# Banded attention and a Sinkhorn mixture of experts: keys loaded in an order in which each query tile's 256 keys are two stretches of 128 adjacent columns

## The chip, the cores and the metric

The kernel runs on one core of one Trainium2 chip. The time is the device time of one execution in microseconds. Runs of an unchanged kernel agree within about 0.1% here (three runs from 2232.98 to 2233.5 us).

## The reference, cut to what matters

```python
# q, k, v: [4, 8, 768, 64] float32; n_global = 8, n_local = 96
scores = (q @ k.T) / sqrt(64)
rel = pos[:, None] - pos[None, :]
is_global = pos[None, :] < n_global
is_local = (rel >= 0) & (rel < n_local)
dist = where(is_global & ~is_local, n_local, abs(rel))
scores = where(is_global | is_local, scores - slope[h] * dist, -1e9)
a = exp(scores - max(scores)); a = a / (sum(a) + 1e-9)
x = a @ v                       # -> [3072, 512]
P = exp(x @ w_gate - max); 8 times: rows to sum 1, columns to sum 1, times N / E
out = sum over e of P[:, e] * (relu(x @ w1[e]) @ w2[e])   # 8 experts, 512 -> 1024 -> 512
```

A query needs only the 96 keys up to itself and the first 8 keys of the sequence. For a tile of 128 queries these lie among the tile's own 128 keys, the last 96 keys of the tile before, and the first 32 keys (`MAX_GLOBAL`, `G` in the code): 256 keys.

## The kernel before, in words

The work of the attention is cut into 32 items. An item is one batch, one half of the sequence (three tiles of 128 queries; half 0 or half 1) and two heads side by side in the 128 columns. Items 0 to 3 are half 0, 4 to 7 half 1, and so on; four items make a unit, and there are eight units. Each item has three groups, one for each query tile, with both heads; the groups are counted through as `t`, 96 in all.

For an item, the queries (three blocks of 128 x 128), the keys and the values are loaded by DMA, all issued from the SP queue (`load_qk`, `load_v`). Even items use a region of the tile `scratch` that is there from the start (`early_raw`), odd items a tile of the pool `f_raw`; so each has one buffer, and the loads of item n+2 wait until item n has used them. `load_pair` lays keys and values out alike. In half 0 there are four blocks: block 0 is made of the first 32 keys and the last 96 of tile 1, blocks 1 to 3 are the three tiles. In half 1 there are six: for each query tile one block of the first 32 keys and the last 96 of the tile before, and one with its own tile. Tiles 0 to 5 of the sequence appear partly twice by that.

`prepare` turns queries and keys: PE transposes each block into a PSUM tile `tp` (line 89 by way of `InOrder`), ACT copies it out as the high part (`qh`, `kh`, L248), DVE subtracts to get the low part (`ql`, `kl`, L249). It runs in three parts: the queries, four key blocks, and in half 1 two more key blocks; after the last part the queries and keys of item n+2 are asked for. `scores` makes three products for each group and head (low and high parts), `softmax` adds the scaled bias table on DVE (L296) and takes the exponential on ACT (L300), `turn` transposes the weights (`t_ps`, copied out on ACT at L322), and `values` multiplies them with the value blocks into `o_ps`. After the third group the values of item n+2 are asked for (`flush`).

The bias tables come from `distances` (DVE, at the very start, before a branch on the values of `n_global` and `n_local`) and `scale_bias`: for each head a table of 128 columns (first tile) and one of 256. Heads 0 and 1 are scaled on DVE, the others on POOL (L159). They lie in the tile `acc`, which the expert part later uses as its accumulator.

PE's order is the program's order. The tile framework sets the order of the other engines and of the SP queue from dependencies and from its own estimate of times. From unit 1 on, `between` mixes work of expert 0 into PE's stream (`filler`: `h_ps`, `y_ps`, stored by way of `y_sb` to `ys`), and POOL prepares operands of the later experts (`oh`, `ol`), which the SP queue stores to `op_m` in DRAM. After about 345 us the attention is over; the rest of the time is expert products with nothing of the attention in them.

The order of the work around the change, in `unit`:

```python
for t in range(u * per, (u + 1) * per, CHUNK):      # CHUNK = 2
    self.ahead(range(t + AHEAD, t + AHEAD + CHUNK))  # scores and softmax of later groups
    self.flush()                                     # values products, load_v(n + 2)
    turned = [(t + c, self.turn(t + c)) for c in range(CHUNK)]
    between(CHUNK)                                   # expert 0, stores
    ...
    for c in range(CHUNK):
        between(1)
        self.prepare(t + AHEAD + NG + 1 + c)         # transposes, load_qk(n + 2)
```

Of the kernel before, what the change touches and what calls it, by code (L numbers as in the profile page):

```python
# [12 lines left out]
ALU = mybir.AluOpType  # L13
# [22 lines left out]
GROUPS = (((0, 0), (1, 0)), ((0, 1), (1, 1)), ((0, 2), (1, 2)))  # L36

# [54 lines left out]
class Banded:  # L92

    SLOTS = 8 * len(GROUPS)
    RAW = UT * P + 4 * UT * P

    SCRATCH = RAW + 2 * P

    def __init__(self, tc, q, k, v, early, scratch):

        self.tc, self.nc = tc, tc.nc
        self.q, self.k, self.v = q, k, v
        self.H, self.D = q.shape[1], q.shape[3]
        H, nb = self.H, 3 * self.H * P
        self.bias1 = early[:, 0:2 * H * P].rearrange("p (h c) -> p h c", h=H)
        self.bias0 = early[:, 2 * H * P:nb].rearrange("p (h c) -> p h c", h=H)
        self.early_raw = scratch[:, 0:self.RAW]
        self.d1 = early[:, nb:nb + 2 * P]  # L110
        self.d0 = early[:, nb + 2 * P:nb + 3 * P]
        self.work = [(b, half, g) for b in range(q.shape[0]) for half in range(2) for g in range(H // 2)]
        self.pending = []
        self.sums, self.inv, self.outs = {}, {}, {}
        self.pe = InOrder(tc)
        nb += 3 * P
        self.early_pT = early[:, nb:nb + 4 * P].rearrange("p (c k) -> p c k", c=4)
        assert nb + 4 * P <= early.shape[1]
        self.warm = scratch[:, self.RAW:].bitcast(mybir.dt.bfloat16)
        self.qk, self.vs, self.ready, self.scored = {}, {}, {}, {}  # L120

    def open(self, ctx, ident, idle):

        tc = self.tc
        self.ident, self.idle = ident, idle
        self.raw = ctx.enter_context(tc.tile_pool(name="f_raw", bufs=1, side="right"))
        self.opd = ctx.enter_context(tc.tile_pool(name="f_opd", bufs=2, side="right"))
        self.wrk = ctx.enter_context(tc.tile_pool(name="f_wrk", bufs=AHEAD + CHUNK, side="right"))
        self.ps = ctx.enter_context(tc.tile_pool(name="f_ps", bufs=2, space=PSUM))

    def distances(self, ng, nl):

        tc, nc, G = self.tc, self.nc, MAX_GLOBAL
        d1, d0 = self.d1, self.d0
        with tc.tile_pool(name="f_tmp", bufs=1) as tmp:
            rel, isl, isg = position_tiles(nc, tmp, P, 0, 2 * P, ng, nl, "d1")
            m = tmp.tile([P, 2 * P], F32, name="m1")
            nc.vector.tensor_scalar(out=m, in0=isl, scalar1=-BIG, scalar2=BIG, op0=ALU.mult, op1=ALU.add)
            nc.vector.tensor_scalar(out=m[:, 0:G], in0=isg[:, 0:G], scalar1=-BIG, scalar2=BIG, op0=ALU.mult, op1=ALU.add)
            nc.vector.tensor_tensor(out=d1, in0=isl, in1=rel, op=ALU.mult)  # L140
            nc.vector.tensor_scalar(out=d1[:, 0:G], in0=isg[:, 0:G], scalar1=nl, scalar2=None, op0=ALU.mult)
            nc.vector.tensor_tensor(out=d1, in0=d1, in1=m, op=ALU.add)
# [4 lines left out]
            nc.vector.tensor_tensor(out=d0, in0=isl, in1=rel, op=ALU.mult)  # L147
            nc.vector.tensor_scalar(out=isl, in0=isl, scalar1=-1.0, scalar2=1.0, op0=ALU.mult, op1=ALU.add)
            nc.vector.tensor_tensor(out=m0, in0=m0, in1=isl, op=ALU.mult)
            nc.vector.tensor_tensor(out=d0, in0=d0, in1=m0, op=ALU.add)  # L150

    def scale_bias(self, g):

        nc, H, D = self.nc, self.H, self.D
        engine = nc.vector if g == 0 else nc.gpsimd
        for h in (2 * g, 2 * g + 1):
            c = -(D ** 0.5) * 2.0 ** (-8.0 * (h + 1) / H)
            for bias, d in ((self.bias0, self.d0), (self.bias1, self.d1)):
                self.tc.keep_in_program_order(engine.tensor_scalar(out=bias[:, h], in0=d, scalar1=c, scalar2=None, op0=ALU.mult))  # L159
# [13 lines left out]
    def raw_tile(self, n, first, width):  # L173


        if n % 2 == 0:
            t = self.early_raw[:, first * UT * P:(first + width) * UT * P]
        else:
            t = self.raw.tile([P, width * UT * P], F32, name=f"raw{width}")
        return t.rearrange("p (t c) -> p t c", c=P)  # L180

    def load_keys(self, dst, src, half, cols):
        nc, D, G = self.nc, self.D, MAX_GLOBAL
        if half == 0:
            nc.sync.dma_start(out=dst[:, 1:1 + UT, cols], in_=src[:, 0:UT])
        else:
            nc.sync.dma_start(out=dst[:, 1::2, cols], in_=src[:, UT:2 * UT])
            nc.sync.dma_start(out=dst[G:, 0::2, cols], in_=src[G:, UT - 1:2 * UT - 1])
            nc.sync.dma_start(out=dst[0:G, 0::2, cols], in_=src[0:G, 0:1].broadcast_to([G, UT, D]))
# [7 lines left out]
    def load_pair(self, dst, src, n):  # L197

        nc, D, G = self.nc, self.D, MAX_GLOBAL
        b, half, g = self.work[n]  # L200
        for t, cols in self.heads(src, n):
            self.load_keys(dst, t, half, cols)
        if half == 0:
            both = src[b, 2 * g:2 * g + 2].rearrange("j s d -> s j d")
            block = dst[:, 0].rearrange("p (j d) -> p j d", j=2)
            nc.sync.dma_start(out=block[0:G], in_=both[0:G])
            nc.sync.dma_start(out=block[G:], in_=both[P + G:2 * P])

    def load_qk(self, n):
# [3 lines left out]
        t = self.raw_tile(n, 0, 3)  # L213
# [3 lines left out]
        self.load_pair(k_r, self.k, n)  # L217
        self.qk[n] = q_r, k_r

    def load_v(self, n):  # L220
        if n >= len(self.work):
            return
        self.vs[n] = self.raw_tile(n, 3, 2)
        self.load_pair(self.vs[n], self.v, n)
# [5 lines left out]
    def prepare(self, t):  # L230
# [3 lines left out]
        if n >= len(self.work):  # L234
            return
        nc = self.nc
        if part == 0:
            self.ready[n] = tuple(self.opd.tile([P, w * UT, P], F32R, name=name)
                                  for name, w in (("qh", 1), ("ql", 1), ("kh", 2), ("kl", 2)))
        q_r, k_r = self.qk[n]  # L240
        qh, ql, kh, kl = self.ready[n]
        nk = self.key_blocks(self.work[n][1])[0]
        src, hi, lo, n0, n1 = ((q_r, qh, ql, 0, UT), (k_r, kh, kl, 0, 4), (k_r, kh, kl, 4, nk))[part]
        if n1 > n0:
            tp = self.turned("tp")
            for t in range(n0, n1):
                self.pe.transpose(out=tp[:, t - n0], in_=src[:, t], identity=self.ident)
            nc.scalar.copy(out=hi[:, n0:n1], in_=tp[:, 0:n1 - n0])  # L248
            nc.vector.tensor_tensor(out=lo[:, n0:n1], in0=tp[:, 0:n1 - n0], in1=hi[:, n0:n1], op=ALU.subtract)  # L249
        if part == 2:  # L250
            self.load_qk(n + 2)

    def scores(self, ts):
# [3 lines left out]
        banks = [self.ps.tile([P, CHUNK, 2 * P], F32, name=f"s_ps{j}", tag=f"s{j}", bufs=1) for j in range(2)]  # L257
        s_lists, terms = [], []
        for c, t in enumerate(ts):
            n, group = divmod(t, len(GROUPS))  # L260
            blocks = self.key_blocks(self.work[n][1])[1]
# [15 lines left out]
    def softmax(self, t, s_list):  # L277
# [5 lines left out]
        blocks = self.key_blocks(half)[1]  # L283
# [6 lines left out]
        for u, (j, i) in enumerate(GROUPS[group]):  # L290
            h = 2 * g + j
            nb = len(blocks[i])
            bias = self.bias0[:, h] if nb == 1 else self.bias1[:, h]
            pv = p_sb[:, u, 0:nb].rearrange("p a c -> p (a c)")
            views.append(pv)
            nc.vector.tensor_tensor_reduce(out=pv, in0=s_list[u], in1=bias, scale=-(D ** -0.5), scalar=3.0e38,  # L296
# [13 lines left out]
    def blocks(self, n, group):  # L310
        slots = self.key_blocks(self.work[n][1])[1]
        return [(u, a, j, i, slots[i]) for u, (j, i) in enumerate(GROUPS[group]) for a in range(len(slots[i]))]

    def turn(self, t):
# [6 lines left out]
        pT = self.wrk.tile([P, 4, P], F32, name="pT", bufs=1) if t % 2 else self.early_pT  # L321
# [668 lines left out]
def kernel(  # L990
# [68 lines left out]
```

## Time and profile before

| | |
|---|---|
| median of three runs | 2233.35 us (2232.98 to 2233.5) |
| the profiled execution | 2235.71 us |
| its span, first to last instruction | 2233.9 us |
| mean granted TensorE clock | 0.990 |
| busy share PE / PEld / DVE / ACT / POOL | 98% / 81% / 61% / 34% / 50% |

PE is the matrix engine, PEld its weight loads, DVE the vector, ACT the scalar, POOL the general engine; SPq is the queue of the SyncE engine, which issues the DMAs. In a row of the timeline stand start and duration in us, engine, line, operation, what is written and read, how many; in brackets the idle time of the engine before it and what ended that. A row of waits reads: who waited, for whom, us in total, how often, the longest. Matmuls overlap, so the spacing of two starts tells more of the cost of one than its duration.

### The profile page before, as it was taken

The page shows a single profiled execution, that of the slowest core. Times are in us where ns is not written, and L with a number is a line of the kernel's source. Part 1 is how long each engine was busy: PE and PEld are TensorE (multiplying, and loading weights), DVE is VectorE, ACT ScalarE, POOL GpSimd, SP SyncE. Part 2 cuts the span into 40 slices and gives each one's busy share as a digit, 9 for nine tenths or more (in the row PEclk, how much of TensorE's full clock was granted, in tenths as well). Part 3 has the DMA queues.
Part 4 walks back from the last instruction along what each step waited for, and adds up shares of the span by engine and source line. Part 5 has one row for each costly group of instructions (what it writes and reads, how often), then busy time and mean ns, then how long its engine had stood idle before and what let it go on. Part 6 is the DMA issues. An engine that isn't in the chain of part 4 may idle for free.

```text
span 2233.9 us, 29587 instructions
## 1 busy us (share of the span) xinstructions
PE 2194.8 (98%) x10887; PEld 1817.9 (81%) x10887; DVE 1358.9 (61%) x2382; ACT 769.0 (34%) x1562; POOL 1126.3 (50%) x1050
## 2 busy tenths in 40 slices
PE   8999998999999999999999999999999999999999
PEld 5888886778888888888888888888888888888887
DVE  5555556866566656655666666566556665666665
ACT  6676763223222322223222222222232232222221
POOL 5575575545454545445544545454555455544540
PEclk8999999999999999999999999999999999999999
DMA  6566554111111111162111111111521111111111
GB/s 157 160 168 180 150 161 162 39 48 48 57 48 57 48 57 48 57 221 89 49 49 55 51 54 48 57 48 57 167 88 47 57 48 57 48 51 54 50 46 49
DMA packets 224842, 177.68 MB, mean 80 GB/s; under 512 B 119728, under 2 KB 187824, under 8 KB 224688
## 3 DMA queue, kind: packets, MB, share of 16 engines
q1 hardware_dynamic: 224688, 175.70, 25.6%
q8 instruction: 87, 1.43, 0.3%
q14 instruction: 67, 0.55, 0.1%
HBM read 146.56 MB, written 29.10 MB: 79 GB/s over the span
## 4 chain that ended last, share of the span: by engine, by line
PE 93%; ACT 3%; DVE 3%; issue 1%; DMA 0%; SPq 0%; DVEq 0%; ACTq 0%
PE y_ps L86 45%; PE bank_a L86 11%; PE bank_d L86 10%; PE bank_c L86 10%; PE bank_b L86 5%; PE h_ps L86 2%; PE o_ps L86 2%; PE t_ps L89 2%; PE s_ps L86 1%; ACT p_sb L300 1%; PE tp L89 1%; DVE kl L249 0%; PE r_ps L89 0%; PE g_ps L86 0%; ACT kh L248 0%
## 5 line engine op out<-in xcount | busy, mean ns | idle before, releaser
L962 DVE SCALAR_TENSOR_TENSOR acc<-y_ps,pm,acc 128x512 f32<-128x512 f32 x672 | 502.7, 748 | 244.5 <-PE y_ps L86 243.3
L545 POOL TENSOR_TENSOR wl<-wsum,wh 128x1280 fp32r<-128x1280 f32 x90 | 266.1, 2957 | 556.2 <-ACT wh L544 556.2
L567 POOL TENSOR_TENSOR wsum<-w1f 128x256 f32<-128x256 f32 x450 | 318.0, 741 | 318.6 <-DMA w1f<-in_moe_w_dram 318.5
L86 PE MATMUL y_ps<-w2h,h_set 128*128 128x512 f32 x1408 | 434.7, 390 | 0.0
L86 PE MATMUL y_ps<-w2h,x 128*128 128x512 f32 x1408 | 433.5, 389 | 0.0
L544 ACT CAST w2h<-w2f 128x1024 fp32r<-128x1024 f32 x90 | 94.8, 1054 | 687.8 <-issue 612.2
L86 PEld LDWEIGHTS y_ps<-w2h,h_set 128*128 128x128 f32 x1408 | 265.2, 188 | 55.2
L86 PEld LDWEIGHTS y_ps<-w2h,x 128*128 128x128 f32 x1408 | 264.3, 188 | 54.9
L86 PE MATMUL y_ps<-w2l,h_set 128*128 128x512 f32 x704 | 274.9, 390 | 3.9 <-DVE acc L962 3.9
L86 PE MATMUL y_ps<-w2l,x 128*128 128x512 f32 x704 | 273.9, 389 | 0.0
L86 PE MATMUL bank_a<-m,wh 128*128 128x512 f32 x696 | 242.8, 389 | 1.0 <-DVE h_set L613 1.0
L545 POOL TENSOR_TENSOR w2l<-w2f,w2h 128x1024 fp32r<-128x1024 f32 x90 | 216.5, 2406 | 53.0 <-ACT w2h L544 53.0
L86 PE MATMUL bank_d<-x,wh 128*128 128x512 f32 x696 | 242.6, 389 | 0.0
L86 PE MATMUL bank_c<-x,wh 128*128 128x512 f32 x696 | 242.5, 389 | 0.0
L652 DVE TENSOR_TENSOR scratch<-scratch,bank_d 128x512 f32<-128x512 f32 x90 | 61.9, 688 | 175.1 <-PE bank_d L86 171.4
L86 PEld LDWEIGHTS y_ps<-w2l,h_set 128*128 128x128 f32 x704 | 132.7, 188 | 31.7 <-DVE acc L962 4.2
L86 PEld LDWEIGHTS y_ps<-w2l,x 128*128 128x128 f32 x704 | 132.1, 188 | 27.4
L86 PEld LDWEIGHTS bank_a<-m,wh 128*128 128x128 f32 x696 | 130.6, 188 | 29.0 <-DVE h_set L613 1.9
L86 PEld LDWEIGHTS bank_c<-x,wh 128*128 128x128 f32 x696 | 130.6, 188 | 27.1
L86 PEld LDWEIGHTS bank_d<-x,wh 128*128 128x128 f32 x696 | 130.6, 188 | 27.0
L86 PE MATMUL bank_a<-m,wl 128*128 128x512 f32 x348 | 135.4, 389 | 0.0
L86 PE MATMUL bank_d<-x,wl 128*128 128x512 f32 x348 | 135.4, 389 | 0.0
(230 smaller groups left out, 3568.4 us busy)
## 6 DMA issues: line engine op xcount, KB each, us to landing
w1f<-in_moe_w_dram SPq DMA_DIRECT2D x92, 512.0 KB, 3.4
w2f<-in_moe_w_dram SPq DMA_DIRECT2D x92, 512.0 KB, 3.6
x<-op_m SPq DMA_DIRECT2D x16, 512.0 KB, 7.9
m<-op_m SPq DMA_DIRECT2D x12, 512.0 KB, 8.1
out_dram<-acc SPq DMA_DIRECT2D x24, 256.0 KB, 4.0
ys<-y_sb SPq DMA_DIRECT2D x21, 256.0 KB, 2.2
acc<-ys SPq DMA_DIRECT2D x21, 256.0 KB, 4.1
op_m<-oh SPq DMA_DIRECT2D x30, 128.0 KB, 1.9
```

The source lines that it names most:

```text
L86: return self.tc.keep_in_program_order(self.engine.matmul(*args, **kw))
L89: return self.tc.keep_in_program_order(self.engine.transpose(*args, **kw))
L300: nc.scalar.activation(out=pv, in_=pv, func=AF.Exp, bias=mx[:, u:u + 1], scale=-1.0, accum_out=sm[:, i, j:j + 1])
L544: self.nc.scalar.copy(out=hi, in_=full)
L545: self.nc.gpsimd.tensor_tensor(out=lo, in0=full, in1=hi, op=ALU.subtract)
L567: nc.gpsimd.tensor_tensor(out=s[:, n], in0=x, in1=y, op=op)
L652: tt(out=t3, in0=t3, in1=d, op=ALU.subtract)
L962: nc.vector.scalar_tensor_tensor(out=a, in0=y_ps, scalar=moe.pm[:, tt, e:e + 1], in1=a, op0=ALU.mult, op1=ALU.add)
```

## The change

Keys are laid down so that each tile's 256 keys are two stretches of 128 adjacent columns after turning (`KEYS` holds where they begin), with no key loaded or turned twice: three blocks in half 0, four in half 1. Within a block the 96 later keys of a tile come first, and 32 earlier ones (of the same tile or the first of the sequence) fill the last 32 places, so that a stretch may begin inside a block, at 96 or 224. `scores` and the bias read two stretches with a step (`runs`). The bias table gets 512 columns a head, in the order of the stretches. Values keep some blocks twice (`VALUES`): four blocks in half 0, five in half 1, because products with the turned weights need all 128 rows of a block. The loads are issued in other pieces: for keys five in half 0 and seven in half 1, for values seven and nine, where before they were four and six for both. `prepare` has two parts instead of three, and `load_qk(n + 2)` follows the second. The raw buffers shrink from 15 to 12 blocks, `pT` gets two buffers of its pool, the table `bias0` moves to the pool `f_raw`, and `acc` and `scratch` become two regions of one tile.

The diff, cut to its core:

```diff
+KEYS = (((0,), (0, 128), (96, 256)), ((0, 128), (128, 256), (224, 384)))
+VALUES = (((0,), (0, 1), (2, 3)), ((0, 1), (1, 2), (3, 4)))
+BIAS = ((None, (32, 256), (128, 352)), ((0, 384), (32, 256), (128, 352)))
...
-    RAW = UT * P + 4 * UT * P
-
-    SCRATCH = RAW + 2 * P
-
-    def __init__(self, tc, q, k, v, early, scratch):
+    QK, V = UT + 4, 5
+    RAW = (QK + V) * P
+    BIAS1 = 4 * P
+
+    SCRATCH = RAW + 3 * P
...
-            nc.vector.tensor_tensor(out=d1, in0=isl, in1=rel, op=ALU.mult)
-            nc.vector.tensor_scalar(out=d1[:, 0:G], in0=isg[:, 0:G], scalar1=nl, scalar2=None, op0=ALU.mult)
-            nc.vector.tensor_tensor(out=d1, in0=d1, in1=m, op=ALU.add)
+            nc.vector.tensor_tensor(out=isl, in0=isl, in1=rel, op=ALU.mult)
+            nc.vector.tensor_scalar(out=isl[:, 0:G], in0=isg[:, 0:G], scalar1=nl, scalar2=None, op0=ALU.mult)
+            for to, c, w in ((P, 0, P), (0, P, G), (G, G, P - G), (2 * P, P + G, P - G), (3 * P - G, P, P), (4 * P - G, 0, G)):
+                nc.vector.tensor_tensor(out=d1[:, to:to + w], in0=isl[:, c:c + w], in1=m[:, c:c + w], op=ALU.add)
...
-            nc.vector.tensor_tensor(out=d0, in0=d0, in1=m0, op=ALU.add)
+            for to, c, w in ((0, G, P - G), (P - G, 0, G)):
+                nc.vector.tensor_tensor(out=d0[:, to:to + w], in0=rel[:, c:c + w], in1=m0[:, c:c + w], op=ALU.add)
...
-            for bias, d in ((self.bias0, self.d0), (self.bias1, self.d1)):
-                self.tc.keep_in_program_order(engine.tensor_scalar(out=bias[:, h], in0=d, scalar1=c, scalar2=None, op0=ALU.mult))
-
-    def key_blocks(self, half):
-
-        if half == 0:
-            return 4, [[1], [1, 2], [0, 3]]
-        return 2 * UT, [[2 * n, 2 * n + 1] for n in range(UT)]
+            for bias, d in ((self.bias0[:, h], self.d0), (self.bias1[:, h * W:(h + 1) * W], self.d1)):
+                self.tc.keep_in_program_order(engine.tensor_scalar(out=bias, in0=d, scalar1=c, scalar2=None, op0=ALU.mult))
+
+    def runs(self, src, places):
+
+        if len(places) == 1:
+            return src[:, places[0]:places[0] + P].unsqueeze(1)
+        step = places[1] - places[0]
+        return src[:, places[0]:places[0] + 2 * step].rearrange("p (a c) -> p a c", a=2)[:, :, 0:P]
+
+    def bias(self, h, half, i):
+        places = BIAS[half][i]
+        if places is None:
+            return self.bias0[:, h:h + 1]
+        return self.runs(self.bias1, [h * self.BIAS1 + c for c in places])
...
-    def load_keys(self, dst, src, half, cols):
-        nc, D, G = self.nc, self.D, MAX_GLOBAL
-        if half == 0:
-            nc.sync.dma_start(out=dst[:, 1:1 + UT, cols], in_=src[:, 0:UT])
-        else:
-            nc.sync.dma_start(out=dst[:, 1::2, cols], in_=src[:, UT:2 * UT])
-            nc.sync.dma_start(out=dst[G:, 0::2, cols], in_=src[G:, UT - 1:2 * UT - 1])
-            nc.sync.dma_start(out=dst[0:G, 0::2, cols], in_=src[0:G, 0:1].broadcast_to([G, UT, D]))
 
     def heads(self, src, n):
 
@@ -194,34 +200,53 @@
         for j in range(2):
             yield src[b, 2 * g + j].rearrange("(t p) d -> p t d", p=P), slice(j * self.D, (j + 1) * self.D)
 
-    def load_pair(self, dst, src, n):
-
-        nc, D, G = self.nc, self.D, MAX_GLOBAL
+    def load_pair(self, dst, src, n, values):
+
+        nc, G = self.nc, MAX_GLOBAL
         b, half, g = self.work[n]
+        W = P - G
+        both = src[b, 2 * g:2 * g + 2].rearrange("j (t p) d -> p t j d", p=P)
+
+        def block(p, w, slot, row, tile):
+
+            nc.sync.dma_start(out=dst[p:p + w, slot].rearrange("p (j d) -> p j d", j=2), in_=both[row:row + w, tile])
+
+        first = 0 if half == 0 else UT
         for t, cols in self.heads(src, n):
-            self.load_keys(dst, t, half, cols)
+            nc.sync.dma_start(out=dst[0:W, half:half + 2, cols], in_=t[G:, first:first + 2])
+        last = half + (3 if values else 2)
         if half == 0:
-            both = src[b, 2 * g:2 * g + 2].rearrange("j s d -> s j d")
-            block = dst[:, 0].rearrange("p (j d) -> p j d", j=2)
-            nc.sync.dma_start(out=block[0:G], in_=both[0:G])
-            nc.sync.dma_start(out=block[G:], in_=both[P + G:2 * P])
+            for t, cols in self.heads(src, n):
+                nc.sync.dma_start(out=dst[W:, 0:2, cols], in_=t[0:G, 0:2])
+            if values:
+                block(0, G, 2, 0, 0)
+                block(G, W, 2, G, 1)
+        else:
+            block(0, G, 0, 0, UT)
+            block(G, W, 0, G, UT - 1)
+            block(W, G, 1, 0, 0)
+            block(W, G, 2, 0, UT + 1)
+            if values:
+                block(0, G, 3, 0, 0)
+                block(G, W, 3, G, UT + 1)
+        block(0, P, last, 0, first + UT - 1)
...
-        self.load_pair(k_r, self.k, n)
+        self.load_pair(k_r, self.k, n, False)
...
-        if n >= len(self.work):
+        if n >= len(self.work) or part == 2:
             return
         nc = self.nc
         if part == 0:
-            self.ready[n] = tuple(self.opd.tile([P, w * UT, P], F32R, name=name)
-                                  for name, w in (("qh", 1), ("ql", 1), ("kh", 2), ("kl", 2)))
+            self.ready[n] = tuple(self.opd.tile([P, w], F32R, name=name)
+                                  for name, w in (("qh", UT * P), ("ql", UT * P), ("kh", 4 * P + MAX_GLOBAL), ("kl", 4 * P + MAX_GLOBAL)))
         q_r, k_r = self.qk[n]
         qh, ql, kh, kl = self.ready[n]
-        nk = self.key_blocks(self.work[n][1])[0]
-        src, hi, lo, n0, n1 = ((q_r, qh, ql, 0, UT), (k_r, kh, kl, 0, 4), (k_r, kh, kl, 4, nk))[part]
-        if n1 > n0:
-            tp = self.turned("tp")
-            for t in range(n0, n1):
-                self.pe.transpose(out=tp[:, t - n0], in_=src[:, t], identity=self.ident)
-            nc.scalar.copy(out=hi[:, n0:n1], in_=tp[:, 0:n1 - n0])
-            nc.vector.tensor_tensor(out=lo[:, n0:n1], in0=tp[:, 0:n1 - n0], in1=hi[:, n0:n1], op=ALU.subtract)
-        if part == 2:
+        src, hi, lo, nb = (q_r, qh, ql, UT) if part == 0 else (k_r, kh, kl, UT + self.work[n][1])
+        tp = self.turned("tp")
+        for t in range(nb):
+            self.pe.transpose(out=tp[:, t], in_=src[:, t], identity=self.ident)
+        tp = tp.rearrange("p t c -> p (t c)")[:, 0:nb * P]
+        nc.scalar.copy(out=hi[:, 0:nb * P], in_=tp)
+        nc.vector.tensor_tensor(out=lo[:, 0:nb * P], in0=tp, in1=hi[:, 0:nb * P], op=ALU.subtract)
+        if part == 1:
             self.load_qk(n + 2)
...
-                blk = blocks[i]
-                ks = slice(blk[0], blk[-1] + 1, max(1, blk[-1] - blk[0]))
-                s_list.append(banks[j][:, c, 0:len(blk) * P])
-                terms.append((s_list[-1], [(a[rows, i], b[rows, ks]) for a, b in ((qh, kl), (ql, kh), (qh, kh))]))
+                places = KEYS[self.work[n][1]][i]
+                s_list.append(banks[j][:, c, 0:len(places)])
+                terms.append((s_list[-1], [(a[rows, i * P:(i + 1) * P], self.runs(b[rows], places))
+                                           for a, b in ((qh, kl), (ql, kh), (qh, kh))]))
...
-            nc.vector.tensor_tensor_reduce(out=pv, in0=s_list[u], in1=bias, scale=-(D ** -0.5), scalar=3.0e38,
+            nc.vector.tensor_tensor_reduce(out=pv, in0=s_list[u], in1=self.bias(h, half, i), scale=-(D ** -0.5), scalar=3.0e38,
...
-        slots = self.key_blocks(self.work[n][1])[1]
+        slots = VALUES[self.work[n][1]]
...
-        pT = self.wrk.tile([P, 4, P], F32, name="pT", bufs=1) if t % 2 else self.early_pT
+        pT = self.wrk.tile([P, 4, P], F32, name="pT", bufs=2)
...
-    acc = const.tile([P, 2 * WT, out.shape[1]], F32, name="acc")
-    scratch = const.tile([P, Banded.SCRATCH], F32, name="scratch")
-    band = Banded(tc, q, k, v, acc.rearrange("p t d -> p (t d)"), scratch)
+    n_acc = 2 * WT * out.shape[1]
+    early = const.tile([P, n_acc + Banded.SCRATCH], F32, name="early")
+    acc = early[:, 0:n_acc].rearrange("p (t d) -> p t d", t=2 * WT)
+    scratch = early[:, n_acc:]
+    band = Banded(tc, q, k, v, early, n_acc)
```

More of the change, by code (lines that the diff above doesn't have):

```diff
@@ L105, in __init__ @@
         self.H, self.D = q.shape[1], q.shape[3]
[L106 to L112, printed above, removed]
+        assert n_bias == self.H * self.BIAS1
+        self.bias1, rest = early, early[:, n_bias:]
+        self.early_raw = rest[:, 0:self.RAW]
+        self.d1 = early[:, n_bias - self.BIAS1:n_bias]
+        self.d0 = rest[:, self.RAW:self.RAW + P]
+        self.warm = rest[:, self.RAW + P:].bitcast(mybir.dt.bfloat16)
+        self.work = [(b, half, g) for b in range(q.shape[0]) for half in range(2) for g in range(self.H // 2)]
         self.pending = []
@@ L256, in scores @@
         nc, D = self.nc, self.D
-        banks = [self.ps.tile([P, CHUNK, 2 * P], F32, name=f"s_ps{j}", tag=f"s{j}", bufs=1) for j in range(2)]
+        banks = [self.ps.tile([P, CHUNK, 2, P], F32, name=f"s_ps{j}", tag=f"s{j}", bufs=1) for j in range(2)]
         s_lists, terms = [], []
```

26 lines of the change are left out of this document (10 added, 16 removed).

## The prediction

> **What bounds the kernel now.** I read the page's busy times first, then the busy times by stretch, then PE's waits, then the DMA queue's timeline, then the chain. Only the attention stretch is touched by the change (first instruction to about 345 us), so only its rows count. First the page, busy time of each engine over the span; then the stretches (us of the stretch, busy us and instructions of PE, PEld, DVE, ACT, POOL, then granted clock, DMA share, GB/s); then all of PE's waits from 66 to 322 us:
>
> ```profile
> span 2233.9 us, 29587 instructions
> PE 2194.8 (98%) x10887; PEld 1817.9 (81%) x10887; DVE 1358.9 (61%) x2382; ACT 769.0 (34%) x1562; POOL 1126.3 (50%) x1050
> ```
> ```profile
> 20.00:66.00 46.00, 39.11 (x308) 31.93 (x309) 25.59 (x97) 34.87 (x114) 24.37 (x25) 0.78 0.72 182
> 66.00:106.00 40.00, 39.56 (x339) 33.67 (x338) 21.24 (x78) 28.52 (x89) 16.02 (x20) 1.00 0.57 152
> sum 240.00, PE 237.70 PEld 203.98 DVE 131.70 ACT 170.65 POOL 146.51; mean PE 39.62 PEld 34.00 DVE 21.95 ACT 28.44 POOL 24.42
> ```
> ```profile
> PE s_ps L86 <- DVE kl L249: 1.3, 5, 0.3
> ```
>
> From 66 us on PE is busy 39.6 of every 40 us and waits 1.3 us in all: there a transpose taken from PE is time taken from the kernel, as long as nothing makes PE wait. From 20 to 66 us no expert work is mixed in yet, the clock is 0.78 and PE has 15% idle: there PE's time is only partly the limit.
>
> The other resource near its limit is the SP queue, which issues every load and store, in order. Its timeline (start, duration of the issue; "..." leaves out rows between): value loads of items 20 and 21, then a query and a key pair. Its waits from 66 to 322 us follow, and the issue counts of what else it carries, with KB and the median time to landing:
>
> ```profile
> 217.65 0.40 SPq L187 DMA_DIRECT2D scratch<-in_v_dram  x1
> ...
> 220.16 0.46 SPq L189 DMA_DIRECT2D scratch<-in_v_dram  x1
> 220.72 0.37 SPq L839 DMA_DIRECT2D ys<-y_sb  x1
> ...
> 225.30 0.46 SPq L189 DMA_DIRECT2D raw<-in_v_dram  x1
> ...
> 232.38 0.92 SPq L216 DMA_DIRECT2D raw<-in_q_dram  x2
> 233.35 1.01 SPq L185 DMA_DIRECT2D raw<-in_k_dram  x2
> 234.40 0.48 SPq L206 DMA_DIRECT2D raw<-in_k_dram  x1
> ```
> ```profile
> SPq L793 <- POOL oh L597: 13.6, 14, 2.4
> SPq L839 <- ACT y_sb L838: 11.9, 6, 3.2
> ```
> ```profile
> ys<-y_sb SPq DMA_DIRECT2D x21, 256.0 KB, 2.2
> op_m<-oh SPq DMA_DIRECT2D x30, 128.0 KB, 1.9
> op_m<-ol SPq DMA_DIRECT2D x30, 128.0 KB, 2.0
> scratch<-in_v_dram SPq DMA_DIRECT2D x32, 96.0 KB, 2.2
> op_m<-oh SPq DMA_DIRECT2D x10, 256.0 KB, 2.2
> op_m<-ol SPq DMA_DIRECT2D x10, 256.0 KB, 2.3
> op_m<-x SPq DMA_DIRECT2D x16, 128.0 KB, 2.0
> op_m<-x SPq DMA_DIRECT2D x8, 256.0 KB, 2.4
> raw<-in_v_dram SPq DMA_DIRECT2D x16, 24.0 KB, 2.0
> ```
>
> Six issues from 217.65 to 220.72 us: 0.51 us for one, with the gap behind it. The four from 232.38 to 234.40 take 0.505 each. An item now issues 2 + 4 + 4 = 10 loads (half 0) or 2 + 6 + 6 = 14 (half 1), 12 on average, and the stores above are 125 over 32 items, 3.9 each: 15.9 issues x 0.51 = 8.1 us of queue for one item. The length of an item comes from the key and query transposes of the odd items, which run from 14.8 to 314.6 us:
>
> ```profile
> L89 PE MATMUL tp<-ident,raw x128: 270/272/384, 14.8 to 314.6; 128*128 128x128 f32 x128
> ```
>
> That is items 1 to 31, 299.8 / 30 = 10.0 us an item. So the queue works 8.1 of 10.0 us, and a good part of the rest it stands in front of a store whose data isn't there (the two rows of waits, 25.5 us).
>
> **The change, part by part.** *Transposes removed.* Half 0 turns 3 key tiles instead of 4, half 1 turns 4 instead of 6: 16 x 1 + 16 x 2 = 48 on PE. What one costs is its spacing and not the 272 ns of its row. From the chain, four at full clock and four in the slow stretch:
>
> ```profile
> 300.86 0.44 PE tp L89 x4
> 36.63 0.66 PE tp L89 x4
> ```
>
> 0.11 us each at full clock, 0.165 early. Items 7 to 31 lie in the full stretch: 2 + 4 + 8 + 4 + 8 + 4 + 8 = 38 transposes, 38 x 0.11 = -4.2 us, on the path. The other 10 are worth 1.65 us at most, nothing at least (where ACT ends the chain); I take -0.8. The smaller copies of the turned keys on ACT (16 of 512 columns become 384, 16 of 256 go) and the subtractions on DVE that follow them are costed at nothing: 28.4 and 22.0 of 40 us busy beside a full PE. The PSUM turn that goes in half 1 frees nothing that PE waits for.
>
> *Loads.* Half 0: keys 4 to 5 issues, values 4 to 7; half 1: keys 6 to 7, values 6 to 9. That is +4 for every item, 128 in all, 65 us of queue at 0.51, although the bytes of the keys fall. An item now asks 19.9 x 0.51 = 10.15 us of a queue that has 10.0 - 0.165 (a mean transpose and a half less) = 9.83 us for it. In half 1 it is 21.9 x 0.51 = 11.17 us against 9.78, so the queue falls back 1.39 us an item, 5.6 us in a unit of four; in half 0 it asks 9.13 and makes up 0.76 an item. PE feels this through the values, whose tile is loaded after the item two before has used it. Their lead now, last issue plus the 2.0 us of the landing row against the first product:
>
> ```profile
> 225.93 0.66 PE L86 MATMUL o_ps<-acc,scratch 128*64 128x128 f32 x8
> ...
> 234.05 0.61 PE L86 MATMUL o_ps<-pT,raw 128*64 128x128 f32 x8
> ```
>
> Item 20: 225.93 - 222.16 = 3.8 us; item 21: 234.05 - 227.30 = 6.7; mean 5.2. Against it stand 5.6 us of backlog and 3 x 0.51 = 1.5 us of longer load: 1.9 us of stall in a unit, 7.6 over four. One thing works against that: 6 of the 9 value issues of half 1 now write blocks that are free one group (3.3 us) earlier, and at best this hides the stall whole, 0. At the other end, 0.525 us an issue (the key pair and its gap, 1.05 for two) gives 4 x (11.5 - 9.78) = 6.9 of backlog, 3.2 of stall, 12.8 in all. I take 6.4, 1.6 a unit: earlier release spreads the issues, but makes no time in a queue that has none. What queues behind a late load: the other items' loads, the y_sb stores (ACT waits for one of two tiles) and the op_m stores (POOL, three tiles); these have more lead than the values and are inside the same bounds.
>
> *Moved.* Queries and keys of item n+2 are asked for one part earlier. In odd items this puts 7 or 9 issues, 3.6 to 4.6 us, ahead of a value load that has 6.7 us of lead; in even items the pair moves out of the way. Nothing for both together, the bound is already in the 12.8.
>
> *Start.* Rows of the queue, of PE, DVE and POOL:
>
> ```profile
> 6.27 0.43 SPq L207 DMA_DIRECT2D scratch<-in_v_dram  x1
> 8.81 0.93 SPq L216 DMA_DIRECT2D raw<-in_q_dram  x2
> ```
> ```profile
> 19.21 0.75 PE L89 MATMUL tp<-ident,scratch 128*128 128x128 f32 x4 [0.32 <-DMA scratch<-in_k_dram]
> 10.29 0.56 DVE L249 TENSOR_TENSOR ql<-tp,qh 128x384 fp32r<-128x384 f32 x1 [0.51 <-ACT qh L248]
> 8.84 0.42 DVE L142 TENSOR_TENSOR acc<-acc,m 128x256 f32<-128x256 f32 x1
> 9.50 0.29 DVE L150 TENSOR_TENSOR acc<-acc,m 128x128 f32<-128x128 f32 x1
> 9.72 4.27 PE L86 MATMUL w_ps<-scratch 128*128 128x512 bf16 x12
> 18.50 0.53 POOL L531 MEMSET ghl<- 128x512 f32 x1
> 24.82 1.04 POOL L554 CAST w1h<-w1f 128x1024 fp32r<-128x1024 f32 x1 [1.94 <-DMA w1f<-in_moe_w_dram]
> ```
> ```profile
> L159 POOL TENSOR_SCALAR acc<-acc 128x256 f32<-128x256 f32 x6 | 5.2, 869 | 0.2
> L159 POOL TENSOR_SCALAR acc<-acc 128x128 f32<-128x128 f32 x6 | 3.2, 530 | 7.7 <-DVE acc L150 7.5
> ```
>
> Four more issues before the branch fit into the 2.1 us between 6.70 and 8.81. After it, key 1, value 1 and key 2 bring 1 + 3 + 1 issues, 2.55 us, ahead of the keys of item 2, for which PE already waits 0.32 us at 19.21. Bounds 0 (ACT ends the chain anyway) and 3.5 (0.9 us more if the queue reaches the branch late); I take +2.0, near the row that shows the wait. The distance tables are written by 8 additions over 640 columns instead of 2 over 384. From 0.42 us for 256 columns and 0.29 for 128, one costs 0.16 us and 1 ns a column: 6 x 0.16 + 0.26 = 1.2 us more on DVE by this estimate. 0.51 of it lies in DVE's idle time, and the split queries it delays are wanted only after the 12 warming products, at 9.72 + 4.27 = 13.99: nothing, 0.7 if that cover is gone. POOL's scaled table of 512 columns instead of 256 takes 2 x (869 - 530) = 0.68 us longer, 4.1 for six: done at 22.6 instead of 18.5 us, before the weights that it waits for until 24.82: nothing.
>
> **Sum.** -4.2 - 0.8 + 2.0 + 6.4 = +3.4 us. The profiled execution took 2235.71 us around its span of 2233.9, 2.4 above the median of 2233.35; the sum is a difference inside it, so the median becomes 2236.8. Ends: -4.2 - 1.65 = -5.9 (2227.5); -4.2 + 3.5 + 12.8 + 0.7 = +12.8 (2246.2).
>
> **Two rules beside the rows.** The row: a load of 24 KB holds the queue 0.46 us, a key load of 96 KB 0.5, so the queue pays by the piece. The Trainium skill, "DMA: Bandwidth & Descriptors", section "Rules for kernel authors", says to leave a transfer over all 128 partitions in one piece and not to split it by partitions; by it this change goes the wrong way, and on the queue the trace agrees. The same page of the Trainium skill, section "Issuing engines are not separate DMA queues", holds the time to start a DMA to be usually small beside the DMA itself; by that rule the 128 issues cost nothing and the sum is that of the first rival. The trace disagrees so far: 8.1 of 10.0 us is not small.
>
> **Rivals.** *The queue absorbs it (faster).* Its waits vanish when it runs late, and the two rows alone give 25.5 us back. Then only the transposes remain: -4.2 - 0.8 = -5.0, 2228.4. Against it: half 1 lacks 1.39 us an item even with no wait at all. *The queue sets the pace (slower).* Value loads of half 1 stall PE 3.2 us a unit: -5.0 + 2.0 + 12.8 = +9.8, 2243.2. It decides once an issue costs 0.52 us or more, or leads are below 4 us; item 20 with 3.8 speaks for it, the earlier release against. *The turned keys were not on the path*, some wait taking their place elsewhere, with a queue that holds: +0, 2233.4; PE's 1.3 us of waits speak against it.
>
> **How the numbers follow.** About 0.2% (4.5 us) is what can be told from no change here. Forecast 0.44: half of its stall range beyond +4.5, so 0.24 same and 0.20 slower. Absorbed 0.28: 0.24 faster, 0.04 same. Queue sets the pace 0.19: slower. Not on the path 0.09: same. Together faster 0.24, same 0.37, slower 0.39. The likeliest alone spans 2231 to 2242. Range for all: 2227.5 below, and above 2247, a little past the upper end, since a stall also delays the stores.
>
> **What would show it.** 208 transposes tp instead of 256, 0.11 us apart. Queue waits for oh and y_sb shrink to a few us. New PE waits at o_ps on the value loads of items 4 to 7 of each eight, none in half 0. PE's keys of item 2 later than 19.2 us. Wrong, if issues of the new pieces run below 0.47 us, if PE shows no wait for in_v_dram, or if the hand-over to the experts after 345 us changes its order.

## Result and profile after

Before 2233.18 us (2232.98 to 2233.5, four runs), after **2254.0 us** (2250.8 to 2256.79, four runs): ratio 1.009, 95% interval 1.0078 to 1.0102. The kernel became slower, outside the predicted range of 2227.5 to 2247. The profiled execution took 2251.36 us around its span; the span grew by 2249.4 - 2233.9 = 15.5 us.

The page's busy times of the changed kernel, against the first fence of the prediction:

```profile
span 2249.4 us, 29632 instructions
PE 2194.9 (98%) x10839; PEld 1815.6 (81%) x10839; DVE 1354.7 (60%) x2372; ACT 763.0 (34%) x1546; POOL 1132.2 (50%) x1050
```

PE has 48 instructions fewer and the same busy time: what the transposes gave back is in it, and so are products that ran at half clock (below). The stretches, as before (us; busy us and instructions of PE, PEld, DVE, ACT, POOL; clock, DMA share, GB/s). The last row is the full stretch, from the first query transpose of item 8 to the last product of o_ps; below it stands the same stretch of the kernel before:

```profile
20.00:66.00 46.00, 37.77 (x320) 30.20 (x319) 24.64 (x95) 35.38 (x117) 12.39 (x12) 0.84 0.48 116
66.00:106.00 40.00, 38.26 (x318) 32.79 (x316) 20.31 (x77) 26.48 (x85) 27.55 (x31) 0.96 0.51 135
74.90:357.20 282.30, 269.60 (x2182) 228.60 (x2179) 136.27 (x488) 180.78 (x550) 171.38 (x201) 0.98 0.54 148
```
```profile
73.60:340.00 266.40, 264.10 (x2217) 226.55 (x2216) 142.18 (x500) 184.72 (x562) 157.37 (x181) 1.00 0.59 162
```

The stretch became 16 us longer with less work in it, and PE idles 12.7 us of it instead of 2.3. PE's waits from 66 to 360 us say on what:

```profile
PE o_ps L89 <- DMA raw<-in_v_dram: 8.3, 6, 3.0
PE o_ps L89 <- DMA early<-in_v_dram: 3.1, 4, 1.1
PE s_ps L89 <- DVE kl L273: 1.8, 7, 0.3
PE tp L92 <- DMA raw<-in_q_dram: 0.5, 1, 0.5
```

The third row is the one that was there before. The others are new: value loads that come late, and once queries. Why they are late stands in the queue's timeline (start, us; L212 loads one block, L216 and L220 pieces of a pair of heads, L241 queries, L813 stores):

```profile
308.17 0.91 SPq L216 DMA_DIRECT2D raw<-in_v_dram  x2
309.12 0.91 SPq L220 DMA_DIRECT2D raw<-in_v_dram  x2
310.08 1.39 SPq L212 DMA_DIRECT2D raw<-in_v_dram  x3
311.56 0.41 SPq L813 DMA_DIRECT2D op_m<-oh  x1
...
316.95 0.96 SPq L241 DMA_DIRECT2D raw<-in_q_dram  x2
317.97 0.97 SPq L216 DMA_DIRECT2D raw<-in_k_dram  x2
318.98 2.36 SPq L212 DMA_DIRECT2D raw<-in_k_dram  x5
321.44 0.42 SPq L813 DMA_DIRECT2D op_m<-oh  x1
321.95 1.46 SPq L813 DMA_DIRECT2D op_m<-ol  x1
```

The queue has no gap: the seven issues that load one value tile take 308.17 to 311.5, and each starts when the one ahead is out. The waits of the queue from 66 to 322 us fit that; the first two rows are its longest, the third is the one for oh:

```profile
SPq L212 <- PE t_ps L92: 2.7, 4, 1.5
SPq L212 <- PE s_ps L89: 2.6, 5, 1.2
SPq L813 <- POOL oh L617: 0.9, 3, 0.5
```

Before, it stood 13.6 and 11.9 us in front of oh and y_sb. Now it is 0.9 for oh, and y_sb has no row: when a store's turn comes, its data is mostly there already.

### The profile page after: what moved, and what is told of

Its sections match the earlier page's. It is cut to its first block, busy times and chain, and to the rows that moved or that the text cites. A ratio compares the mean times of both kernels' runs of the same rounds, so it can differ in the third digit from the quotient of the medians.

```text
span 2249.4 us, 29632 instructions
## 1 busy us (share of the span) xinstructions
PE 2194.9 (98%) x10839; PEld 1815.6 (81%) x10839; DVE 1354.7 (60%) x2372; ACT 763.0 (34%) x1546; POOL 1132.2 (50%) x1050
## 4 chain that ended last, share of the span: by engine, by line
PE 92%; DVE 2%; ACT 2%; DMA 2%; SPq 1%; issue 1%; POOL 1%; POOLq 0%; ACTq 0%; DVEq 0%
PE y_ps L89 44%; PE bank_a L89 10%; PE bank_c L89 10%; PE bank_d L89 10%; PE bank_b L89 5%; PE h_ps L89 2%; PE t_ps L92 2%; PE o_ps L89 2%; PE s_ps L89 1%; PE tp L92 1%; ACT p_sb L320 1%; DMA raw<-in_v_dram 1%; PE g_ps L89 0%; PE r_ps L92 0%; PE y_ps L698 0%
## 5 line engine op out<-in xcount | busy, mean ns | idle before, releaser
L982 DVE SCALAR_TENSOR_TENSOR early<-y_ps,pm,early 128x512 f32<-128x512 f32 x672 | 503.1, 749 | 243.7 <-PE y_ps L89 243.1
L672 DVE TENSOR_TENSOR early<-early,bank_d 128x512 f32<-128x512 f32 x90 | 61.8, 687 | 173.0 <-PE bank_d L89 172.0
L89 PE MATMUL bank_c<-x,wl 128*128 128x512 f32 x348 | 135.4, 389 | 0.0
```

Of the source, the lines that this page charges most:

```text
L89: return self.tc.keep_in_program_order(self.engine.matmul(*args, **kw))
L672: tt(out=t3, in0=t3, in1=d, op=ALU.subtract)
L982: nc.vector.scalar_tensor_tensor(out=a, in0=y_ps, scalar=moe.pm[:, tt, e:e + 1], in1=a, op0=ALU.mult, op1=ALU.add)
```

## Experiments

All are read in the same way from their traces: when item 8 starts, how long the full stretch is, how long PE idles in it, what follows it to the end of the span ("rest"), and the issues of the SP queue in the stretch with the share of it that they fill (sum of their spacings: start to next start where the queue goes straight on, otherwise the issue's own duration and 0.05 us). Each ratio is against the kernel before, run beside it.

| kernel | item 8 | stretch | PE idle | rest | issues, share | median us | ratio, 95% |
|---|---|---|---|---|---|---|---|
| before | 73.6 | 266.3 | 2.3 | 1894.0 | 403, 80% | 2233.18 | |
| after | 74.9 | 282.3 | 12.7 | 1892.2 | 514, 97% | 2254.0 | 1.0078-1.0102 |
| values_few | 70.4 | 261.6 | 2.1 | 1890.4 | 431, 88% | 2222.89 | 0.9932-0.9965 |
| keys_few | 67.6 | 261.6 | 2.1 | 1891.3 | 424, 86% | 2222.97 | 0.9936-0.9968 |
| stores_pool | 75.3 | 261.7 | 2.1 | 1901.7 | 408, 85% | 2240.21 | 1.0019-1.0039 |
| stores60_only | 76.1 | 261.6 | 2.1 | 1891.7 | 454, 94% | 2229.55 | 0.9971-0.999 |
| relief | 69.1 | 261.6 | 2.1 | 1889.1 | 453, 93% | 2223.75 | 0.9942-0.997 |
| loads01_only | 69.4 | 281.1 | 12.1 | 1894.8 | 512, 97% | 2247.24 | 1.0042-1.0076 |
| qk_late | 69.3 | 288.4 | 17.4 | 1891.2 | 524, 97% | 2251.87 | 1.0065-1.0097 |
| before_split2 | 74.2 | 287.8 | 13.6 | 1894.2 | 466, 95% | 2257.14 | 1.0086-1.012 |
| before_split4 | 84.7 | 324.0 | 37.2 | 1896.0 | 516, 98% | 2305.63 | 1.0305-1.034 |
| before_relief | 68.2 | 266.4 | 2.3 | 1892.8 | 348, 69% | 2229.8 | 0.9974-0.9992 |

The theory was the prediction's rival "the queue sets the pace" (Q): too many issues on SP, whichever they are. Against it stood: the smaller pieces, landing late by themselves (P); the value loads alone, by their place and release (V); the queries and keys asked for one part earlier (M); and all else that came with the change, key order, bias pieces, the shared tile (O).

**Fewer value loads (values_few).** In `load_pair` of the changed kernel:

```diff
+        if values:
+            for t, cols in self.heads(src, n):
+                nc.sync.dma_start(out=dst[:, c:c + UT, cols], in_=t[:, first:first + UT])   # c = half
+            for slot in ((3,) if half == 0 else (0, 4)):
+                block(0, G, slot, 0, first)
+                block(G, W, slot, G, first)
+            return
```

> The changed kernel, but the values are loaded in 4 issues (half 0) and 6 (half 1), as many as before the change, with plain tiles in their places; the rows of the value blocks then don't match the order of the weights, so the output is not the reference's, while every product and its size stay. The SP queue gets 16.9 issues an item instead of 19.9. Theory Q (the queue is full: 0.54 us an issue, 18.6 issues in the 10.0 us of an item, and the values come late): 16.9 fit, the stalls at o_ps vanish and the transposes' gain is left, 2228 to 2232 us. Theory P (the transfers of small pieces themselves land late): the keys keep their pieces, the values don't, so most of the loss goes as well: 2230 to 2236. Theory O (the new order of keys, the bias in two stretches, the merged tile or the earlier request for keys cost the time): nothing changes, 2250 to 2257.

```profile
70.40:332.00 261.60, 259.50 (x2181) 222.36 (x2179) 135.96 (x488) 179.26 (x550) 171.16 (x200) 1.00 0.57 158
```

2222.89 us, lower than expected. The stretch fell by 20.7 us to 261.6 at full clock, with the same transposes and products as after. Theory O has nothing left to explain. The miss of 5 us lies ahead of the stretch and behind it: item 8 starts 3.2 us before the kernel before has it, and the rest is 3.6 us shorter; the expectation had only the stretch.

**Fewer key loads (keys_few).**

```diff
+        if not values:
+            for t, cols in self.heads(src, n):
+                nc.sync.dma_start(out=dst[:, half:half + UT, cols], in_=t[:, first:first + UT])
+            if half == 1:
+                block(0, P, 0, 0, first)
+            return
```

> The changed kernel with its value loads as they are (7 and 9 pieces), but the keys come as plain tiles in 2 issues (half 0) and 3 (half 1) instead of 5 and 7; the order of keys is then wrong and the output not the reference's, every product keeps its size. 16.4 issues an item. Theory Q (the total of the SP queue decides, whichever load it carries): as with the short value loads, the stretch from item 8 to the last product falls from 282 to 262 us, the time to 2222 to 2230. Theory V (the values in 7 and 9 pieces are late by themselves, each load being longer than its lead): PE still waits for in_v_dram, 2245 to 2257.

```profile
PE s_ps L89 <- DVE kl L279: 1.3, 5, 0.3
```

That is the only wait of PE from 66 to 345 us: the value loads, cut as in the changed kernel, are no longer late once some key loads are gone. The stretch is 261.6 again. So it is the number of issues, not what the value loads do: V falls.

**Stores on POOL's queue (stores_pool).** All 104 stores and copies of the operand pairs that the expert work sends to op_m:

```diff
-                dma(*spills.pop(0))
+                to, of = spills.pop(0)
+                nc.gpsimd.dma_start(out=to.bitcast(F32), in_=of.bitcast(F32))
```

> The changed kernel with all its load pieces, but the 104 stores to op_m are issued by POOL instead of the SP queue: 16.6 issues an item are left on SP. Theory Q: the stalls at o_ps go, 2228 to 2233 us, some us more if the issuing delays POOL's own work. Theory P: the pieces are as small as ever and land as late, 2248 to 2257. Theory O: 2250 to 2257.

The stretch was mended as expected (261.7), but the time was 2240.21, because the rest grew to 1901.7. PE's waits behind 66 us show where:

```profile
PE c_ps L761 <- DVE pm L758: 19.0, 3, 9.4
```

The hand-over to the experts waits 19.0 us. In the changed kernel the same wait is 11.6 us. stores60_only, below, keeps the last 20 stores of oh and ol and the 24 copies on SP and has a rest of 1891.7; so it is some of these 44 that cost more on POOL, and which of them no run separates.

**The kernel before, with loads cut in two (before_split2, before_split4).** The old key order and all 256 transposes, but the large loads in two pieces of 64 partitions, for the values only (64 issues more), and for keys and values (128 more, as in the change); the edit, cut to half 0:

```diff
-            nc.sync.dma_start(out=dst[:, 1:1 + UT, cols], in_=src[:, 0:UT])
+            for p in (slice(0, 64), slice(64, P)):
+                nc.sync.dma_start(out=dst[p, 1:1 + UT, cols], in_=src[p, 0:UT])
```

> The kernel before, with its own order of keys, but each value load of three tiles is cut into two of 64 partitions: 2 issues more an item, 17.9 in all, the same bytes. Theory Q: 17.9 x 0.54 = 9.7 us of 10.0, the queue just holds with some late loads in half 1 (19.9 issues): 2233 to 2240 us. Theories P and O: P a little slower, 2233 to 2236; O unchanged, 2233.

> The kernel before, with its own order of keys, but each load of three tiles of keys and of values is cut into two of 64 partitions: 4 issues more an item, 128 in all, as many as the change added, with the same bytes and no transpose removed. Theory Q: 19.9 x 0.54 = 10.75 us an item against 10.0, 0.75 x 30 = 22 us: 2250 to 2260, with PE waiting for in_v_dram at o_ps. Theory P: pieces of 48 KB are no smaller than some of before, 2233 to 2238. Theory O: 2233.

2257.14 and 2305.63 us: both slower, in the direction that the queue theory gives, and far beyond its sizes. PE's waits of before_split4 are the new kind of wait again, at o_ps and now at the keys' transposes too:

```profile
PE o_ps L86 <- DMA scratch<-in_v_dram: 22.5, 19, 2.8
PE tp L89 <- DMA scratch<-in_k_dram: 14.3, 6, 3.7
```

Its queue shows why the sizes were off (L186 is the cut load, L208 and L209 the blocks that follow it, unchanged):

```profile
217.36 0.61 SPq L186 DMA_DIRECT2D scratch<-in_v_dram  x1
218.01 0.60 SPq L208 DMA_DIRECT2D scratch<-in_v_dram  x1
218.66 0.43 SPq L209 DMA_DIRECT2D scratch<-in_v_dram  x1
```

A piece of 64 partitions takes 0.61 us to issue (median of L186), against 0.43 to 0.48 for the whole load before (medians of L185), and the unchanged block behind it 0.60 instead of 0.48. So these two kernels add queue time, with the same bytes and products, to the kernel before, and it stalls PE alike; as a measure of the change's issues they are too dear, since its own pieces take 0.41 to 0.47 (medians of L212, L216 and L220).

**Queries and keys asked for later again (qk_late).**

```diff
-        if n >= len(self.work) or part == 2:
+        if n >= len(self.work):
+            return
+        if part == 2:
+            self.load_qk(n + 2)
             return
...
-        if part == 1:
-            self.load_qk(n + 2)
```

> The changed kernel, but load_qk(n + 2) stands after the third part as before the change, so queries and keys are asked for one part later. 19.9 issues an item as in the change. Theory Q: a full queue stays full whatever the order, 2248 to 2260 us. Theory M (the earlier request pushes the value loads of the odd items back, and that is the loss): the value loads go first again, 2235 to 2245.

2251.87 us, as the queue theory has it. The start became earlier (69.3), the stall stayed (stretch 288.4, PE idle 17.4 us): the order only moves where PE waits. M falls.

**Relief of the queue (relief).** The changed kernel whole, but with the value loads of items 0 and 1 and the first 60 of the 80 stores of oh and ol issued by POOL:

```diff
+        queue = nc.gpsimd if values and n < 2 else nc.sync      # in load_pair, for its loads
...
-                dma(*spills.pop(0))
+                to, of, own = spills.pop(0)                     # own: a store of oh or ol
+                sent[0] += own
+                engine = nc.gpsimd if own and sent[0] <= 60 else nc.sync
+                engine.dma_start(out=to.bitcast(F32), in_=of.bitcast(F32))
```

> The changed kernel with all its load pieces; the first 60 of the 80 stores of oh and ol, and the value loads of items 0 and 1, are issued by POOL, so that SP carries 14 issues less at the start and about 18 an item after it; the last 20 stores stay on SP, to leave POOL free before the experts take over. Theory Q: start about 3 us shorter, middle stretch 262 to 266 us, rest 1892: 2222 to 2232, faster than both kernels at best. Theory V or O: 2245 to 2257.

```profile
69.10:330.70 261.60, 259.46 (x2182) 222.30 (x2179) 135.93 (x488) 179.23 (x550) 202.47 (x260) 1.00 0.57 161
```
```profile
PE s_ps L89 <- DVE kl L274: 1.3, 5, 0.3
```

2223.75 us, faster than both kernels, with every load and transpose of the change. The second row is PE's only wait from 66 to 345 us. The same issues at the same sizes, 60 stores of them on another queue while the attention runs, and the loss of 20.7 us is gone. P falls with it, and by the landing rows too: from 75 to 330 us the 48 KB value pieces land as soon after their issue in the changed kernel (first row) as in the relieved one (second row). They are issued late, and not carried slowly.

```profile
raw<-in_v_dram SPq DMA_DIRECT2D x40, 48.0 KB, 1.9
raw<-in_v_dram SPq DMA_DIRECT2D x46, 48.0 KB, 2.0
```

**The same relief without the change (before_relief).** The two edits in the kernel before:

> The kernel before with the same relief: the first 60 stores of oh and ol and the value loads of items 0 and 1 issued by POOL. Its queue is at 80% in the middle stretch, where PE has no idle time. Theory Q: only the start gets shorter, by 0 to 3 us: 2229 to 2234, and slower than the relieved change by the transposes' 4 us. Theories V, O and M say nothing of it but 2229 to 2234 as well.

2229.8 us. Its stretch does not move (266.4: nothing waited there), but item 8 starts 5.4 us earlier, more than the 0 to 3 expected: the start of the kernel before was held back by the queue as well. Against it, relief is 6.0 us faster; 4.8 of that is the stretch.

**Each half of the relief (loads01_only, stores60_only).**

> The changed kernel; only the value loads of items 0 and 1 go to POOL, 14 issues less before the keys of item 2. Theory Q: the start gets as short as in the relieved kernel (first query of item 8 at 69 us instead of 75), but the queue is as full as ever after it, and what the start gains is given back, because the queue only waits less: 2247 to 2254 us.

> The changed kernel; only the first 60 of the 80 stores of oh and ol go to POOL. Theory Q: the middle stretch falls to 262 us, the start stays at 75 us: 2226 to 2232. If the long wait at the hand-over that the run with all 104 stores on POOL showed (PE waiting 19 us for the Sinkhorn step) comes from the late stores on POOL, it is gone here; if it comes from any store on POOL, 2236 to 2242.

2247.24 and 2229.55 us. The early loads on POOL mend the start (69.4) and leave the queue of the stretch full (281.1); the stores mend the stretch (261.6) and leave the start (76.1). Each half does its own part of what relief does in start and stretch. By the table's shares, PE does not stall in the full stretch with the queue 93 or 94% full, and stalls at 95%.

## Why the prediction was wrong, step by step

The working had the right mechanism, a queue that falls behind and values that come late by it, and one term far too small.

*Transposes in the full stretch, -4.2: right.* 261.6 against 266.3 is -4.7 where nothing stalls. The tile's instructions and the chain of the changed kernel:

```profile
L92 PE MATMUL tp<-ident,early x104: 270/272/474, 8.8 to 317.9; 128*128 128x128 f32 x104
L92 PE MATMUL tp<-ident,raw x104: 270/272/418, 13.1 to 331.1; 128*128 128x128 f32 x104
```
```profile
206.86 0.33 PE tp L92 x3
207.71 0.44 PE tp L92 x4
```

208 of them, 0.11 us apart. The rival "not on the path" is out.

*Start and early transposes, -0.8 + 2.0: the sum agrees, in part by luck.* Item 8 starts at 74.9 against 73.6, +1.3. The wait that the +2.0 stood for came: PE's timeline shows the keys of item 2 at 21.26 instead of 19.21 and its queries now waiting too, and a stall for comparison:

```profile
19.83 0.88 PE L92 MATMUL tp<-ident,early 128*128 128x128 f32 x3 [3.24 <-DMA early<-in_q_dram]
21.26 1.02 PE L92 MATMUL tp<-ident,early 128*128 128x128 f32 x3 [0.55 <-DMA early<-in_k_dram]
...
134.17 0.84 PE L89 MATMUL o_ps<-pT,raw 128*64 128x128 f32 x4 [2.97 <-DMA raw<-in_v_dram]
```

But before 74.9 us PE also stood for the values of items 3 and 5, which the sum did not have in this part:

```profile
PE o_ps L89 <- DMA raw<-in_v_dram: 3.6, 2, 2.2
```

What made up for these 3.6 us isn't separated; the clock from 20 to 66 us, 0.84 instead of 0.78, may be part of it.

*Tables, smaller copies, POOL and DVE at nothing, and the hand-over: nothing speaks against them.* None of them has a run of its own. The rest is 1.8 us shorter, which the sum didn't have.

*Stall on the value loads, +6.4 with bounds 0 and 12.8: this step failed.* It measured 282.3 - 261.6 = **20.7 us**. Together: -4.7 + 1.3 + 20.7 - 1.8 = +15.5, the growth of the span. Three things were wrong in it.

First, each unit of half 1 was given a fresh lead of 5.2 us, as if half 0 always restored it. The working's own figures deny that: half 1 falls back 5.6 us in a unit, and half 0 makes up 0.76 an item, 3.0 a unit. Nor was the lead 5.2: by the landings in the trace of the kernel before it is 4.0 and 5.6 us in items 20 and 21, and 2.4 and 2.8 in items 12 and 28. The price made it worse: 0.51 us for an issue was a value from undisturbed rows. The mean spacing of the kernel before was there to be read, 211.9 us for 403 issues, 0.526; 15 issues of over 0.7 us make the difference. In 7 of these the trace has a wait that ended inside the issue, for the other 8 it names nothing. After, it is 272.9 / 514 = 0.531 (the last two rows of the queue's timeline above show an ordinary 0.42 and a long 1.46). At 0.53 an item of half 1 lacks 21.9 x 0.53 - 9.78 = 1.8 us, 7.3 a unit, and one of half 0 gains 9.89 - 17.9 x 0.53 = 0.4, 1.6 a unit: the backlog is never worked off. On average an item asks 19.9 x 0.53 = 10.55 of 9.83 us, and 0.72 x 26 items of the stretch is 18.7, near the 20.7. With the item length of the relieved kernel, 9.95 us (its query transposes of items 8 and 31 start at 69.12 and 297.87), it is 0.60 x 26 = 15.6, so the size is met only roughly. By this account, in a queue that is over its capacity the leads are spent once, and from then on every missing microsecond is PE's. These sums were made with the result known.

Second, "none in half 0" falls with it. In items 9 to 11, 17 to 19 and 25 to 27, all of half 0, the last piece of the values lands after the first product, and in items 11, 19 and 27 PE stands for them, longest at item 11, the 2.97 us above.

Third, the sum had no price for the clock. PE's idle stretches and the 3.4 us behind each, in the changed kernel:

```profile
131.20:134.20 3.00, 0.03 (x1) 0.06 (x2) 1.38 (x7) 1.49 (x6) 0.39 (x1) 0.91 0.32 71
134.20:137.60 3.40, 3.40 (x16) 2.90 (x17) 0.00 (x0) 1.45 (x4) 0.00 (x0) 0.57 0.76 254
179.30:181.00 1.70, 0.01 (x2) 0.01 (x1) 1.14 (x7) 1.70 (x8) 0.00 (x0) 1.00 0.31 68
181.00:184.40 3.40, 3.31 (x18) 2.69 (x19) 0.04 (x1) 1.13 (x5) 0.00 (x0) 0.57 0.56 166
236.90:239.50 2.60, 0.55 (x6) 0.22 (x4) 1.30 (x8) 2.08 (x8) 2.52 (x4) 1.00 0.57 163
239.50:242.90 3.40, 3.40 (x19) 3.07 (x20) 0.00 (x0) 0.58 (x1) 3.16 (x6) 0.50 0.68 181
309.80:311.10 1.30, 0.03 (x1) 0.06 (x2) 1.30 (x7) 1.30 (x6) 1.30 (x2) 1.00 0.26 58
311.10:314.50 3.40, 3.40 (x14) 2.82 (x15) 0.07 (x1) 1.47 (x6) 0.78 (x2) 0.51 0.64 195
```

After each, PE is full but at about half its clock: 3.4 x (0.43 + 0.43 + 0.50 + 0.49) = 6.3 us lost. With 12.7 - 2.1 = 10.6 us of added idle time that makes 16.9 of the 20.7. The other 3.8 lie in PE's busy time (269.60 against 259.46 us in the relieved kernel), and no run separates them. Nor does a run show the same queue at full clock, where PE might have waited that much longer instead: that the clock adds to the loss is argued, not shown.

*What would have shown it wrong.* The pieces take 0.48 from one start to the next (308.17 to 310.08, four of them), PE waits for in_v_dram, the queue's waits for oh and y_sb shrank: all as foretold. "The queue absorbs it" is out for this queue, and is what relief makes true. The rival that came about had a chance of 0.19 and a bound of 12.8 that stood on the same fresh lead; its own condition, 0.52 us an issue, was met by the mean of the kernel before.

The growth of the median, 20.8 us, is 5 more than that of the span, because of the executions that were profiled: that of the changed kernel, 2251.36, is 2.6 below its median (the others took 2250.8, 2256.64 and 2256.79), and that of the kernel before, 2235.71, is 2.5 above. The runs of the changed kernel differ by 6 us. Those of the kernel before differ by 0.5 in the first comparison, but by 5.4 over the 39 runs beside the experiments (2231.59 to 2236.95), which is 0.24% and not the 0.1% given at the head; what makes them differ is open.

By the rule of the Trainium skill in "DMA: Bandwidth & Descriptors", section "Issuing engines are not separate DMA queues", issuing from several engines saves only the sequencer's time for starting a DMA, usually small beside the DMA itself. For a single issue the trace agrees: 0.41 to 0.47 us, with 1.9 us to landing. For the sum it does not: with 74 issues on POOL the time is 2223.75 instead of 2254.0 us.

## What to carry to other kernels

Count the issues of a queue that carries nearly everything, price them at the mean spacing of a long stretch and not at the best rows, and compare that with the time per item: at some 95% and above, in these kernels, the engine that waits pays for further issues, and no lead helps for long. Splitting loads to save work elsewhere is worth it only with a second queue for part of them; here that turned +0.9% into -0.4%, where the same relief alone gives the kernel before -0.2%. Give the other queue what is early and has slack, and be wary of giving it what is issued last before a hand-over.

## Hardware that was not expected

- An idle PE of 1.3 or 1.7 us was followed by some 3.4 us at half clock (fence above). But 2.76 us in qk_late, below, were not: the 3.4 us behind them ran at 1.00. So the length of the gap alone doesn't decide; what else does, these runs don't show. The Trainium skill, "TensorE: Matmul & The Clock Gate", section "Why this matters for your kernels", tells to avoid idle gaps over about 3 us between matmul bursts; in this case gaps of 1.3 and 1.7 us had a drop of the clock behind them, and one of 2.76 us had none.

```profile
128.98:131.74 2.76, 0.00 (x1) 0.03 (x1) 1.39 (x7) 1.50 (x6) 0.00 (x0) 1.00 0.38 96
131.74:135.15 3.41, 3.41 (x23) 2.89 (x24) 0.05 (x1) 2.14 (x7) 0.00 (x0) 1.00 0.60 171
```

- The price of an issue depends on its form and on the one ahead: 0.61 us for 64 partitions, and 0.60 instead of 0.48 for an unchanged load right behind it, while the change's pieces of 96 and 32 partitions took 0.41 to 0.47. Why is not known from these runs.
- Stores issued by POOL cost the stretch nothing visible (60 of them: 261.6 us), though POOL's busy time in it grew from 171.16 us in values_few, with all stores on SP, to 202.47, some 0.5 us a store by this difference. With all 104 on POOL the rest was 10 us longer (1901.7 against 1891.7).
